# Linear attention and a gated MLP on one core: another order of norm multiplies, keys and gate differences in slabs 1 and 2, and of the Silu table load

## The chip, the cores and the metric

The kernel runs on one core of a Trainium2 chip. The metric is device time in microseconds (us), from the first to the last instruction of one launch, as the median of three runs. The profile is one execution of the same program; its span, 272.4 us, is a little shorter than the timed runs.

The engines that matter here are TensorE (PE, the matmuls, with PEld for its weight loads), VectorE (DVE), ScalarE (ACT, activations and copies), GpSimd (POOL) and SyncE (SP), whose queue issues most of the DMA transfers.

## The reference

Attention without a score matrix: the queries are normalized along the head dimension, the keys along the sequence, and keys times values is a 64x64 matrix for each head. A two-layer MLP with a gate `h * sigmoid(beta * h)` follows.

```python
def _attn_ref(q, k, v):                      # (8, 8, 576, 64) each
    q_s = np.exp(q - np.max(q, axis=-1, keepdims=True))
    q_s = q_s / (np.sum(q_s, axis=-1, keepdims=True) + 1e-09)
    k_s = np.exp(k - np.max(k, axis=2, keepdims=True))
    k_s = k_s / (np.sum(k_s, axis=2, keepdims=True) + 1e-09)
    kv = np.einsum('bhsd,bhse->bhde', k_s, v)
    return np.einsum('bhsd,bhde->bhse', q_s, kv)

def _moe_ref(x, w_in, w_out, beta):          # x (4608, 512), d_ff 2048
    h = x @ w_in
    g = h * (1.0 / (1.0 + np.exp(-beta * h)))
    return g @ w_out
```

(The listing writes exp and the subtraction of the maximum in one line; the inputs are 0.1 times normal values. The MLP's x is the attention output with the heads side by side.)

## The kernel before

The program is a list of operations, each given to an engine; `add` works out which earlier operations it must wait for, from the data that it reads (`r`), writes (`w`) and the PSUM banks that it touches. Operations of one engine run in the order in which they are listed. So the place of a call in the Python text is its place in the engine's queue.

The 4608 tokens are worked in nine slabs of 512: slab t for t = 0 to 7 is the first 512 tokens of batch t, and slab 8 the rest of all batches. In a slab, the first pass makes h from XT and WIN in 16 tiles of 128 features (64 matmuls); ScalarE applies Silu to each, and VectorE divides by beta (`scale_g`, line 767). The second pass multiplies by WOUT. It saves an eighth of the work with seven products in place of eight, for which it needs sums and differences of halves of the gates (`g_sum1`, `g_sum2`, `g_diff`).

Beside slab t's products, the attention of batch t + 1 is done. Here are its parts that matter: the norm of the queries (reduction, reciprocal, multiply), the DMA that transposes the result, the keys times values, and the product of both, `quad`.

```python
        def norm_main(b, hp0, n, eng=DVE, sums=True, mult=True):
            i = b % 2
            a = bass.AP(EQ[i], hp0 * 512, [[2048, 128], [64, 8 * n], [1, 64]])
            s_ = bass.AP(QS[i], hp0 * 8, [[32, 128], [1, 8 * n]])
            v_ = bass.AP(QI[i], hp0 * 8, [[32, 128], [1, 8 * n]])
            vb = bass.AP(QI[i], hp0 * 8, [[32, 128], [1, 8 * n], [0, 64]])
            ks = [("eq", i, hp) for hp in range(hp0, hp0 + n)]
            if sums:
                add(DVE, lambda e: e.tensor_reduce(s_, a, AX.X, ALU.add), r=ks,
                    w=[("qs", i, hp0)])
                add(DVE, lambda e: e.reciprocal(v_, s_), r=[("qs", i, hp0)], w=[("qi", i, hp0)])
            if mult:
                add(eng, lambda e: e.tensor_tensor(a, a, vb, ALU.mult), r=ks + [("qi", i, hp0)],
                    w=ks)
        # ... cut ...
        def kvd_t(b, c, n, bk):
            i = b % 2
            a = bass.AP(PS[bk], 0, [[512, 128], [256, n], [1, D]])
            rc = bass.AP(RC[i], c, [[NHP, 128], [1, n], [0, D]])
            add(DVE, lambda e: e.tensor_tensor(KVD[kd(b)][:, c:c + n, 0:D], a, rc, ALU.mult),
                r=[("ps", bk)] + [("rc", i, h2) for h2 in range(c, c + n)],
                w=[("kvd", kd(b), h2) for h2 in range(c, c + n)], bank=[bk])
        # ... cut: kv_steps(b, hps) issues PE's products of EK and VB, and then on VectorE:
                    c, k_ = hps[0], len(hps)
                    s_ = bass.AP(PS[bk], D, [[512, 128], [256, k_]])
                    add(DVE, lambda e: e.reciprocal(RC[i][:, c:c + k_], s_),
                        r=[("ps", bk)], w=[("rc", i, h2) for h2 in hps], bank=[bk])
                    if tiled(b):
                        kvd_t(b, c, k_, bk)
                        return
        # ... cut: quad(b, gs) makes XT for two (or four) of the four head pairs on PE (line 554) ...
            for x in sorted(b_x):
                eng, bk = (DVE, ACTE)[x % 2], b_x[x]
                add(eng, lambda e, eng=eng, x=x, bk=bk: (
                    e.copy if eng == ACTE else e.tensor_copy)(XT[i][:, x, :], PS[bk][:, :]),
                    r=[("ps", bk)], w=[("xt", i, x)], bank=[bk])
        # ... cut ...
        def turn(b, hp0, n):
            i = b % 2
            o = bass.AP(QT[i], hp0 * 512, [[2048, 128], [128, 4 * n], [1, 128]])
            a = bass.AP(EQ[i], hp0 * 512, [[2048, 128], [1, 512 * n]])
            add(SP, lambda e: e.dma_start_transpose(o, a),
                r=[("eq", i, hp) for hp in range(hp0, hp0 + n)],
                w=[("qt", i, hp) for hp in range(hp0, hp0 + n)], slot=f"tq{i}{hp0}")
        # ... cut ...
        def norm_turn(b, hp0):
            norm_main(b, hp0, 2, POOL)
            turn(b, hp0, 2)
        # ... cut ...
        def attn_late(b):
            if b < 4:
                return [(100 if b == 2 else 97, steps(kv_all, b)), (118, one(quad, b, (0,)))]
            return [(96, steps(kv_all, b)), (99, lambda: g_diff(1)), (112, one(quad, b))]
```

PE's matmuls for `quad` wait for KVD and for QT, so for the multiply as well, through the transpose. The gate differences are done in place on VectorE:

```python
        def g_diff(fh):
            f, th = NG * fh, 1 - fh
            add(DVE, lambda e: e.tensor_tensor(gv(f, th, NG), gv(f, th, NG), gv(f, 1 - th, NG),
                                               ALU.subtract),
                r=gk(f, 0, NG) + gk(f, 1, NG), w=gk(f, th, NG), war=True)
```

The second pass, with `at(n)` as the places at which a slab's hooks are called. `tick` counts PE's progress in the slab: 64 in the first pass, then 32/56 for each matmul of the second, so that product n (from 0) begins at 64 + 9.14 n. What `todo` holds is issued when its count is reached.

```python
            at(0)
        # ... cut ...
            prod_s(range(0, 6))
            prod(z5, *gs2(0), *wo(1, 1), True, False, range(0, 6))
            prod_s(range(6, NG))
            prod(z5, *gs2(0), *wo(1, 1), True, False, range(6, NG))
            add(DVE, lambda e: e.tensor_copy(TS[:, :], PS[s][:, :]), r=[("ps", s)], w=["ts"],
                bank=[s])
            at(1)
            add(DVE, lambda e: e.tensor_tensor(TS[:, :], TS[:, :], PS[z5][:, :], ALU.subtract),
                r=["ts", ("ps", z5)], w=["ts"], bank=[z5])
            at(2)
            prod(z2, *gs2(1), *wo(0, 0), True)
        # ... cut: VectorE subtracts z2 from TS (line 922) ...
            if t > 3:
                g_diff(0)
                g_diff(1)
            at(3)
            prod(z5, *gt(0, 0), *wo(0, 1), False)
            copy(z5, 0, 1, ACTE)
            at(4)
            prod(z2, *gt(NG, 1), *wo(1, 0), False)
            copy(z2, 1, 0, ACTE)
            at(5)
            prod(z5, *gt(0, 1), *wsum(1), False, True)
            last(z5, 1, 1)
            at(6)
            prod(z2, *gt(NG, 0), *wsum(2), False, True)
            last(z2, 0, 0)
            at(7)
```

`g_diff(0)` writes what the product after `at(5)` reads, `g_diff(1)` what the product after `at(6)` reads. z5 and z2 are two PSUM banks: a product can start in one of them when the copy before it has read it.

What a slab holds in `todo` (the second half of `quad` comes in the next slab, after its first product), and the hooks of slabs 1, 2 and 3 with `diffs_norm`:

```python
            elif t < 4:
                todo = attn_late(t + 1)
                if t > 1:
                    todo += [(1.5, one(quad, t, (1,)))]
        # ... cut ...
            def diffs_norm(b):
                norm_main(b, 2, 2, mult=False)
                g_diff(0)
                g_diff(1)
                norm_main(b, 2, 2, sums=False)
                turn(b, 2, 2)
        # ... cut ...
            if t == 1:
                on(0, exps, 2)
                on(0, casts, 2)
                on(2, norm_turn, 2, 0)
                on(3, diffs_norm, 2)
                on(3, load, 4)
            elif t == 2:
                on(0, exps, 3)
                on(2, norm_turn, 3, 0)
                on(3, diffs_norm, 3)
                on(3, load, 5)
                on(4, exp_q, 4)
                on(4, casts, 4)
                on(6, norm_turn, 4, 0)
            elif t == 3:
        # ... cut ...
                on(3, g_diff, 0)
                on(4, norm_turn, 5, 0)
                on(5, norm_turn, 5, 2)
```

ScalarE's Exp and Silu lie in different function tables. A load is put in ahead of the first activation that needs the other table; in slabs 1 and 2 the first Silu after the Exps is that of the next slab's first tile.

Of the kernel before, what the change touches and what calls it, by code (L numbers as in the profile page):

```python
# [7 lines left out]
ACT = mybir.ActivationFunctionType  # L8
# [21 lines left out]
PE, ACTE, DVE, POOL, SP = "tensor", "scalar", "vector", "gpsimd", "sync"  # L30
# [14 lines left out]
class Program:  # L45
# [12 lines left out]
    def add(self, eng, fn, r=(), w=(), bank=(), slot=None, after=(), war=False):  # L58
        op = Op(eng, fn, slot)
        op.pos = len(self.ops)  # L60
        deps = op.deps
        deps.extend(after)
        for k in r:
            deps.extend(self.writer.get(k, ()))
            self.readers.setdefault(k, []).append(op)
        for k in w:
            for d in self.readers.get(k, ()):
                if d is not op and (war or not self._same(d, op)):
                    deps.append(d)
            for d in self.writer.get(k, ()):  # L70
                if not self._same(d, op):
                    deps.append(d)
            self.readers[k] = []
            self.writer[k] = [op]
        for k in bank:
            t = self.touch.setdefault(k, {})
            for e, d in t.items():
                if e != eng:
                    deps.append(d)
            t[eng] = op  # L80
        if eng == POOL and slot is None:
            if self.pool is not None:
                deps.append(self.pool)
            self.pool = op
        self.ops.append(op)
        return op
# [72 lines left out]
def bass_efficient_attn_shen__then__act_swish_beta_kernel(  # L159
# [12 lines left out]
    with ExitStack() as es:  # L172
        def sb(name, shape, dt):
            return es.enter_context(nc.sbuf_tensor(name, shape, dt))
# [42 lines left out]
        WARM = sb("WARM", [128, 512], BF16)  # L217
        DUMMY = sb("DUMMY", [128, 8], F32)
# [7 lines left out]
        add = P.add  # L226
# [6 lines left out]
            r=["ts"], w=["idb"])  # L233
        add(POOL, lambda e: e.tensor_scalar(IDF[:, :], TS[0:NF, 0:NF], 0.0, None, ALU.is_equal),
            r=["ts"], w=["idf"])
        add(ACTE, lambda e: e.dma_start(BT[:, :], bass.AP(beta_h, 0, [[128, NF], [1, 128]])),
            w=["bt"], slot="bt")
        add(ACTE, lambda e: e.activation(DUMMY[:, 0:1], WARM[:, 0:1], ACT.Exp), r=["warm"],
            w=["dummy"])
# [109 lines left out]
# [14 lines that stand above are left out]
# [239 lines left out]
# [7 lines that stand above are left out]
# [14 lines left out]
        def one(fn, *a):  # L623
            return lambda: fn(*a)

        def steps(fn, *a):
            return lambda: go(fn(*a))
# [7 lines left out]

        def attn_late(b):
            if b < 4:
                return [(100 if b == 2 else 97, steps(kv_all, b)), (118, one(quad, b, (0,)))]
            return [(96, steps(kv_all, b)), (99, lambda: g_diff(1)), (112, one(quad, b))]

        def spread(steps, lo, hi):
# [9 lines left out]
        def go(steps):  # L651
            for s in steps:
                s()
# [18 lines left out]
        def load_wout(c):  # L672
# [11 lines left out]
            r=[("ps", bb)], w=["bc0"], bank=[bb])  # L684
        add(DVE, lambda e: e.scalar_tensor_tensor(BC[:, :], PS[bb][:, 0:NF], 1e-20, BC[:, :],
                                                  ALU.is_lt, ALU.mult),
            r=[("ps", bb), "bc0"], w=["bc"], bank=[bb])
        add(DVE, lambda e: e.scalar_tensor_tensor(BETA[:, :], BC[:, :], 4e-20, PS[bb][:, 0:NF],
                                                  ALU.mult, ALU.add),
            r=["bc", ("ps", bb)], w=["beta"], bank=[bb])  # L690
# [8 lines left out]
        for c in range(4):  # L699
# [33 lines left out]
            w=["dummy"])  # L733
# [57 lines left out]
        def gv(f, th, n):  # L791
            return GT[:, f:f + n, 256 * th:256 * th + 256]

        def gk(f, th, n):
            return [("gt", f + x, th) for x in range(n)]
# [12 lines left out]
# [5 lines that stand above are left out]
# [140 lines left out]
        for t in range(NSLAB):  # L953
            todo = []
            if t == 0:
                todo = [(x, steps(t_steps, 1, (hp,), NOW, ACTE))
                        for hp, x in enumerate((97, 106, 114, 119))]
                todo += [(107, one(exp_kr_s, 1))]
                todo += [(x, one(exp_k, 1, hp, 1)) for hp, x in enumerate((108, 115, 120, 125.5))]
                todo += [(x, one(cast_v, 1, hp, DVE))  # L960
                         for hp, x in ((1, 118.5), (2, 123), (3, 127))]
                todo += [(x, steps(kv_steps, 1, (hp,), NOW))
                         for hp, x in enumerate((118, 122, 126))]
                todo += [(x, steps(out_step, 1, hp, NOW, ACTE)) for hp, x in enumerate((122.5, 125))]
                todo += [(117, one(o2_evac, 0, 0, 3, ACTE))]
                todo += [(2, steps(out_step, 0, 3, HEAD, DVE))]
# [4 lines that stand above are left out]
                if t == 3:  # L971
                    todo += [(4, one(norm_turn, 4, 2))]
                if t == 1:
                    todo += [(1, steps(out_step, 1, 2, (3,), ACTE)),
                             (3, steps(kv_steps, 1, (3,), (7,))),
                             (6, steps(out_step, 1, 3, (7,), DVE)),
                             (6.1, one(w_sum, 2, 4, 4)), (6.2, one(w_diff, 0)),
                             (6.3, one(w_diff, 1))]
            elif t < 7:
                todo = attn(t + 1)  # L980
            elif t == 7:
                todo = spread(outr_steps(1), 32, 48)
# [31 lines left out]
            if t == 0:  # L1014
# [17 lines left out]
                while todo:  # L1032
# [4 lines left out]
                    r=["warm"], w=["dummy"])  # L1037
# [4 lines left out]
            def on(n, fn, *a):  # L1042
                hooks.setdefault(n, []).append(lambda: fn(*a))
# [4 lines left out]
                if b % 2 == 0:  # L1048
                    exp_kr(b)

            def diffs_norm(b):
                norm_main(b, 2, 2, mult=False)
                g_diff(0)
                g_diff(1)
                norm_main(b, 2, 2, sums=False)
                turn(b, 2, 2)

            def casts(b):
                g = P.writer[("gs2", NG - 1)]
# [5 lines left out]
            if t == 1:  # L1065
                on(0, exps, 2)
                on(0, casts, 2)
                on(2, norm_turn, 2, 0)
                on(3, diffs_norm, 2)
                on(3, load, 4)  # L1070
            elif t == 2:
                on(0, exps, 3)
                on(2, norm_turn, 3, 0)
                on(3, diffs_norm, 3)
                on(3, load, 5)
                on(4, exp_q, 4)
                on(4, casts, 4)
                on(6, norm_turn, 4, 0)
            elif t == 3:
                on(0, exp_k, 4)  # L1080
                on(0, exp_kr, 4)
                on(0, exp_q, 5)
# [3 lines that stand above are left out]
                on(4, exp_qr, 1)  # L1086
                on(5, exp_k, 5)
                on(5, norm_turn_rem)
                on(5, casts, 5)
                on(5, load, 6)  # L1090
                on(7, load_rem, "qrf", qt_h, QRF, 4)
            elif t + 2 < B:
                b = t + 2
                on(0, exps, b)
                on(0, casts, b)
                if t == 4:
                    on(0, load, 7)
                on(3, norm_turn, b, 0)
                on(4, norm_turn, b, 2)
# [40 lines left out]
```

## Time and profile before

| | |
|---|---|
| time, median of 3 | 274.03 us |
| lowest, highest | 273.77, 274.29 us |
| profile's span | 272.4 us |
| PE busy | 262.3 us (96%) |
| DVE busy | 193.9 us (71%) |
| ACT busy | 180.8 us (66%) |
| POOL busy | 58.8 us (22%) |
| granted PE clock | 1.000 |

The profile names an instruction by its line in the kernel and by what it writes and reads, with the numbers of buffers left out: `L361 POOL TENSOR_TENSOR EQ<-EQ,QI` is a norm multiply on GpSimd, `L361 DVE ...` one on VectorE, `L810 DVE ... GT<-GT` a gate difference, `L606 SPq DMA_TRANSPOSE QT<-EQ` the issue of a transpose. A group's idle time is the time in which its engine did nothing just before it, with the operation that ended it as the releaser. A busy time with xN is of N instructions taken together; neighbours on one engine overlap by up to 0.1 us. PE's records overlap more, since matmuls are pipelined.

Over the kernel's span ScalarE makes 16 table loads of 1283 ns each: six ahead of a Silu of line 744, six ahead of an Exp of line 319, and four single ones.

### The profile page before, as it was taken

Reading aid. Unit: us, or ns where it says so; the run is one execution under the profiler, and the core shown is the slowest. Engines: PE = TensorE matmul, PEld = TensorE weight load, DVE = VectorE, ACT = ScalarE, POOL = GpSimd, SP = SyncE. Lnnn points to the kernel's source line nnn. Section 1 sums busy time; section 2 is a strip of 40 time slices with the busy share of each in tenths; the row PEclk is TensorE's granted clock in tenths of the full one; section 3 lists DMA queues with packets and bytes.
Section 4 is the critical chain, followed back from the end, with each engine's and each line's share of the span. In section 5 each row is a group of like instructions: output and inputs, shape, how many; then the busy total and the mean of one; then the engine's idle time right before and its main releaser. Section 6 shows DMA issues by size and latency. Waiting matters only on the chain.

```text
span 272.4 us, 4985 instructions
## 1 busy us (share of the span) xinstructions
PE 262.3 (96%) x1974; PEld 163.5 (60%) x1993; DVE 193.9 (71%) x409; ACT 180.8 (66%) x287; POOL 58.8 (22%) x78
## 2 busy tenths in 40 slices
PE   8999999999899989999999999999999999999994
PEld 2444454448744864468645874587458745874683
DVE  4964586887958798868778885888488549625762
ACT  4898568789277955887778938893783387018610
POOL 2790010006130086100820651036000100000000
PEclk9999999999999999999999999999999999999999
DMA  7999999989799228960399899603600130012005
GB/s 219 318 201 207 227 326 350 288 236 370 157 328 285 82 42 231 293 211 2 63 261 298 252 359 162 193 1 79 213 2 0 22 154 0 2 58 99 0 2 155
DMA packets 59367, 45.95 MB, mean 169 GB/s; under 512 B 28608, under 2 KB 58320, under 8 KB 58320
## 3 DMA queue, kind: packets, MB, share of 16 engines
q1 hardware_dynamic: 54480, 40.90, 53.8%
q0 software_dynamic: 4240, 4.19, 9.3%
q10 hardware_dynamic: 624, 0.53, 0.6%
q8 instruction: 16, 0.26, 0.4%
q14 instruction: 7, 0.06, 0.1%
HBM read 36.71 MB, written 9.44 MB: 169 GB/s over the span
## 4 chain that ended last, share of the span: by engine, by line
PE 81%; DVE 12%; DMA 2%; SPq 2%; issue 1%; ACT 0%; DVEq 0%
PE PS L406 48%; PE PS L844 30%; DVE QS L357 3%; DMA VF<-in_v_dram 2%; DVE GT L810 2%; DVE EQ L361 2%; PE PS L554 1%; PE PS L482 1%; SPq L278 1%; SPq L290 1%; DVE QI L359 1%; DVE O2S L892 1%; DVE VB L377 1%; DVE TS L913 1%; DVE TS L916 1%
## 5 line engine op out<-in xcount | busy, mean ns | idle before, releaser
L406 PE MATMUL PS<-XT,WIN 128*128 128x512 bf16 x560 | 125.4, 379 | 1.5 <-issue 0.3
L744 ACT ACTIVATE GT<-PS,BETA 128x512 bf16<-128x512 f32 x144 | 95.0, 689 | 37.4 <-PE PS L406 37.2
L406 PEld LDWEIGHTS PS<-XT,WIN 128*128 128x128 bf16 x576 | 55.0, 98 | 65.2 <-DVE XT L596 1.1
L767 DVE TENSOR_SCALAR GT<-GT,RB 128x512 bf16<-128x512 bf16 x144 | 52.5, 386 | 38.4 <-ACT GT L744 37.7
L844 PE MATMUL PS<-WOUT,GS 128*128 128x256 bf16 x256 | 31.1, 273 | 0.0
L361 POOL TENSOR_TENSOR EQ<-EQ,QI 128x1024 bf16<-128x1024 bf16 (+1 forms) x11 | 20.0, 1822 | 50.5 <-DVE QI L359 50.2
L844 PE MATMUL PS<-WOUT,GT 128*128 128x256 bf16 x256 | 29.8, 273 | 0.0
L844 PE MATMUL PS<-WSUM,GT 128*128 128x256 bf16 x256 | 29.8, 273 | 0.0
L880 ACT COPY O2S<-PS 128x512 f32<-128x512 f32 (+1 forms) x17 | 9.4, 560 | 27.6 <-PE PS L844 27.6
L844 PEld LDWEIGHTS PS<-WSUM,GT 128*128 128x128 bf16 x256 | 24.8, 98 | 3.7 <-issue 0.9
L844 PEld LDWEIGHTS PS<-WOUT,GT 128*128 128x128 bf16 x256 | 24.8, 98 | 2.9
L844 PEld LDWEIGHTS PS<-WOUT,GS 128*128 128x128 bf16 x256 | 24.8, 98 | 3.0
L319 ACT ACTIVATE EQ<-QF 128x512 bf16<-128x512 f32 x32 | 17.9, 619 | 7.5 <-DMA QF<-in_q_dram 7.4
L803 DVE TENSOR_TENSOR GS<-GT 128x512 bf16<-128x512 bf16 (+2 forms) x32 | 21.9, 685 | 0.0
L377 POOL CAST VB<-VF 128x512 bf16<-128x512 f32 x24 | 16.4, 682 | 25.4 <-DVE GS L803 13.2
L810 DVE TENSOR_TENSOR GT<-GT 128x2048 bf16<-128x2048 bf16 x16 | 20.3, 1301 | 0.0
L357 DVE TENSOR_REDUCE QS<-EQ 128x16 f32<-128x1024 bf16 (+1 forms) x20 | 19.7, 985 | 0.7 <-ACT EQ L319 0.7
L319 ACT ACTIVATE EK<-KF 128x512 bf16<-128x512 f32 x32 | 18.1, 620 | 0.2 <-DMA KF<-in_k_dram 0.2
L892 DVE TENSOR_TENSOR O2S<-TS,PS 128x512 f32<-128x512 f32 (+1 forms) x17 | 10.7, 644 | 9.3 <-PE PS L844 9.3
L844 PE MATMUL PS<-WSUM,GS 128*128 128x256 bf16 x128 | 16.6, 273 | 0.0
L406 PE MATMUL PS<-WOUT,GT 128*128 128x512 bf16 x62 | 15.0, 379 | 0.1
L844 PEld LDWEIGHTS PS<-WSUM,GS 128*128 128x128 bf16 x128 | 12.5, 98 | 3.2
(88 smaller groups left out, 211.2 us busy)
## 6 DMA issues: line engine op xcount, KB each, us to landing
out_dram<-O2S SPq DMA_DIRECT2D x8, 1024.0 KB, 5.0
QF<-in_q_dram SPq DMA_DIRECT2D x6, 1024.0 KB, 6.7
KF<-in_k_dram SPq DMA_DIRECT2D x6, 1024.0 KB, 9.3
VF<-in_v_dram SPq DMA_DIRECT2D x6, 1024.0 KB, 12.5
KF<-in_k_dram SPq DMA_DIRECT2D x8, 256.0 KB, 5.5
VF<-in_v_dram SPq DMA_DIRECT2D x8, 256.0 KB, 5.5
WOUT<-in_moe_w_out_dram POOLq DMA_DIRECT2D x4, 512.0 KB, 16.4
WIN<-in_moe_w_in_dram POOLq DMA_DIRECT2D x3, 512.0 KB, 9.1
```

What stands on the lines that cost most here:

```text
L319: add(ACTE, lambda e, o=o, a=a: e.activation(o, a, ACT.Exp), r=[(name + "f", i, hp)], w=[("e" + name, i, hp)])
L357: add(DVE, lambda e: e.tensor_reduce(s_, a, AX.X, ALU.add), r=ks, w=[("qs", i, hp0)])
L361: add(eng, lambda e: e.tensor_tensor(a, a, vb, ALU.mult), r=ks + [("qi", i, hp0)], w=ks)
L377: add(eng, lambda e: (e.copy if eng == ACTE else e.tensor_copy)(o, a), r=[("vf", i, hp), ("vone", i)], w=[("vb", i, hp)], after=after)
L406: add(PE, lambda e: e.matmul(o, l, r_, start=start, stop=stop), r=r, w=w, bank=[bk])
L744: add(ACTE, lambda e: e.activation(GT[:, f, :], PS[bk][:, :], ACT.Silu, scale=BETA[:, f:f + 1]), r=[("ps", bk), "beta"], w=[("gt", f, 0), ...
L767: add(DVE, lambda e: e.tensor_scalar(GT[:, f, :], GT[:, f, :], RB[:, f:f + 1], None, ALU.mult), r=k + ["rb"], w=k)
L803: add(DVE, lambda e: e.tensor_tensor(GS2[:, i:i + n, :], GT[:, i:i + n, :], GT[:, i + NG:i + NG + n, :], ALU.add), r=[k_ for f in (i, i + ...
L810: add(DVE, lambda e: e.tensor_tensor(gv(f, th, NG), gv(f, th, NG), gv(f, 1 - th, NG), ALU.subtract), r=gk(f, 0, NG) + gk(f, 1, NG), w=gk(f ...
L844: add(PE, lambda e, l=l, r_=r_, st=st, u=u, i=i, b_=b_: e.matmul(PS[b_][:, 256 * u:256 * u + 256], l, r_, start=st, stop=end and i == NG - ...
L880: add(eng, lambda e, b_=b_, u0=u0, u1=u1: (e.copy if eng == ACTE else e.tensor_copy)(o[:, u0:u1, :], bank3(b_)[:, u0:u1, :]), r=[("ps", b_ ...
L892: add(DVE, lambda e, b_=b_, u0=u0, u1=u1: e.tensor_tensor(o[:, u0:u1, :], ts[:, u0:u1, :], bank3(b_)[:, u0:u1, :], ALU.add), r=["ts", ("ps ...
```

## The change

In slabs 1 and 2, VectorE now does the reductions and reciprocals of all four head pairs and the first gate difference, and no multiply; both multiplies of the norm go to GpSimd. The keys (`kv_all`: reciprocals and scaling into KVD) then come on VectorE ahead of the second gate difference, which moves into the list of `attn_late`, right after them. It is meant to bring KVD, and with it `quad`, earlier, by taking work out of VectorE's queue ahead of it.

A dummy activation with Silu is put in at `at(4)`, so that the table is loaded there, ahead of the output copy that follows, and not ahead of the next slab's first Silu. In slab 2 it comes after the four Exps of batch 4's queries. Slab 3 and all later ones have the same operations in the same order as before.

```diff
--- before.py
+++ after.py
@@ -635,7 +635,9 @@
 
         def attn_late(b):
             if b < 4:
-                return [(100 if b == 2 else 97, steps(kv_all, b)), (118, one(quad, b, (0,)))]
+                x = 100 if b == 2 else 97
+                return [(x, steps(kv_all, b)), (x + .1, lambda: g_diff(1)),
+                        (118, one(quad, b, (0,)))]
             return [(96, steps(kv_all, b)), (99, lambda: g_diff(1)), (112, one(quad, b))]
 
         def spread(steps, lo, hi):
@@ -1048,12 +1050,9 @@
                 if b % 2 == 0:
                     exp_kr(b)
 
-            def diffs_norm(b):
-                norm_main(b, 2, 2, mult=False)
-                g_diff(0)
-                g_diff(1)
-                norm_main(b, 2, 2, sums=False)
-                turn(b, 2, 2)
+            def silu_table():
+                add(ACTE, lambda e: e.activation(DUMMY[:, 2:3], WARM[:, 0:1], ACT.Silu),
+                    r=["warm"], w=["dummy"])
 
             def casts(b):
                 g = P.writer[("gs2", NG - 1)]
@@ -1066,14 +1065,18 @@
                 on(0, exps, 2)
                 on(0, casts, 2)
                 on(2, norm_turn, 2, 0)
-                on(3, diffs_norm, 2)
+                on(3, norm_turn, 2, 2)
+                on(3, g_diff, 0)
+                on(4, silu_table)
                 on(3, load, 4)
             elif t == 2:
                 on(0, exps, 3)
                 on(2, norm_turn, 3, 0)
-                on(3, diffs_norm, 3)
+                on(3, norm_turn, 3, 2)
+                on(3, g_diff, 0)
                 on(3, load, 5)
                 on(4, exp_q, 4)
+                on(4, silu_table)
                 on(4, casts, 4)
                 on(6, norm_turn, 4, 0)
             elif t == 3:
```

## The prediction

> **What bounds the kernel now.** I read the page first. In its busy times TensorE (PE) is busy for 262.3 us of 272.4, at a granted clock of 1.000, so all that a change of order can win back is the time in which PE stands still. Then I listed PE's waits over the whole span, and PE's timeline in the second passes of slabs 1 and 2 (60.9 to 75.3 us and 89.7 to 104.8 us). Columns: start, length, engine, line, what; the bracket is the idle time ahead of it and what ended it.
>
> ```profile
> 73.05 0.41 PE L554 MATMUL PS<-QT,KVD 64*64 64x512 bf16 x4 [0.97 <-DVE KVD L459]
> ...
> 102.47 0.41 PE L554 MATMUL PS<-QT,KVD 64*64 64x512 bf16 x4 [1.55 <-DVE RC L490]
> ...
> 106.82 3.41 PE L406 MATMUL PS<-XT,WIN 128*128 128x512 bf16 x15 [0.23 <-DVE XT L596]
> ```
>
> The three gaps, 0.97 + 1.55 + 0.23 = 2.75 us, are the whole prize. The first two stand before the first half of `quad` (L554), which needs both KVD (keys times values, scaled on VectorE) and QT (the transposed query factors, brought by DMA). The chain of waits through slab 2 shows why KVD is late: the two gate differences (L810) and the norm multiply (L361) stand ahead of it on VectorE (DVE).
>
> ```profile
> 97.65 2.72 DVE GT L810 x2
> 100.37 1.55 DVE EQ L361
> 101.92 0.09 DVE RC L490
> ...
> 102.04 0.29 DVE KVD L459
> 102.33 0.09 DVE RC L490
> ```
>
> Last I looked at the other input, QT, in the waits of two stretches, 72 to 74 us (first fence) and 101 to 103 us (second).
>
> ```profile
> PEld PS L554 <- DMA QT<-EQ: 1.2, 1, 1.2
> PE PS L554 <- DVE KVD L459: 1.0, 1, 1.0
> ```
>
> ```profile
> PEld PS L554 <- issue: 1.8, 1, 1.8
> PE PS L554 <- DVE RC L490: 1.5, 1, 1.5
> ```
>
> This is the reading that my number hangs on. In slab 1 the weight load of `quad` waited for the transposing DMA: it was issued at 68.92 and took 4.1 us to land, so at 73.02; KVD was done at 72.77 + 0.29 = 73.06. **Two inputs arrive within 0.05 us of each other**, and the change moves one of them. In slab 2 the transpose was issued at 97.77 and landed 3.1 us later, at 100.87, so there KVD alone holds PE.
>
> **What the skill says.** "SBUF — State Buffer", section "SBUF: two separate sides", says that VectorE and GpSimd share one port pair under an exclusive lock: a VectorE operation with two SBUF inputs, or in a 2-port mode, and a GpSimd operation shut each other out for a whole instruction. The trace agrees. POOL is GpSimd; the two lines are of POOL's and DVE's timelines:
>
> ```profile
> 108.32 1.90 POOL L361 TENSOR_TENSOR EQ<-EQ,QI 128x1024 bf16<-128x1024 bf16 x1 [0.65 <-DVE QI L359]
> ```
>
> ```profile
> 108.61 1.75 DVE L767 TENSOR_SCALAR GT<-GT,RB 128x512 bf16<-128x512 bf16 x1 [0.44 <-ACT GT L744]
> ```
>
> The scaling that takes 386 ns on average took 1.75 us, and ended as the GpSimd multiply did. "ScalarE: Activation LUTs", section "What ACT_TABLE_LOAD costs", puts a switch at 2.66 us with its drain; here the load is 1.28 us and the next activation follows at once (120.25 to the first Exp at 121.55: 1.30), so I use 1.30. Its section "Table sets: the hidden batching unit" says that cheap functions such as copy are in every set; the trace agrees: the copies of L880 run after Exp and those of L771 between Silus with no load of their own.
>
> **The change part by part.**
>
> *1. The multiply leaves DVE.* In each of slabs 1 and 2 one multiply of 128x1024 goes: 1.14 us of the chain in slab 1 (1.21 with overlap), 1.55 in slab 2 (there it waited behind a GpSimd cast). On GpSimd the same shape takes 1.90 us (four of them, 67.0 to 108.3).
>
> *2. The second difference goes behind the keys.* That takes another 1.15 us from ahead of KVD. The tail of reciprocals and scalings is unchanged: 72.25 to 73.06 in slab 1, so 0.81 us, once started.
>
> *3. New order in slab 1.* Up to 68.80 (end of the second reciprocal L359) nothing differs. GpSimd's first multiply ends at 68.90, as before. The first difference starts at 68.72, ahead of the second multiply, which can start some 0.1 us after the first; so I take it that DVE gets the port first, and ends at 69.98 as before. Keys: from 69.9 plus 0.9 to 70.8. The second multiply held the port from 69.9 for 1.85 us to 71.75; the second difference then runs until about 72.85. KVD is thus 2.2 us earlier, **but QT still lands at 73.02**, since the first multiply and the first transpose haven't moved. `quad` starts at 73.05 as before. The second difference at 72.85 is in time for the last product, which started at about 73.5. **Gain of slab 1: 0.** (The second transpose is issued at about 71.8 in place of 72.28; nobody waits for that.)
>
> *4. New order in slab 2.* The reciprocal ends at 97.65. First difference, with the port, to 98.82 (as now). Keys to 99.65. The second multiply blocked until 98.75, then to 100.6. The second difference from 100.6 to 101.7. GpSimd's casts, now behind the multiply, run from 100.7 on and end at about 105.6 in place of 104.4, ahead of the next multiply; that one is not urgent. `quad` needs KVD (99.65), QT (100.87) and PE's own fifteen products before it (from 99.13, 1.80 long: 100.93). So it starts at about 101.0 in place of 102.47: 1.45 us earlier.
>
> *5. What then holds the last product.* After `quad` (0.35) and one product of the sixth group PE would reach the last group at about 101.45. It needs the second difference (101.7) and its PSUM bank, which is free when ScalarE's second output copy has read it. Here is ScalarE (ACT) in slab 2 before:
>
> ```profile
> 98.29 2.19 ACT L319 ACTIVATE EQ<-QF 128x512 bf16<-128x512 f32 x4
> 100.38 0.57 ACT L880 COPY O2S<-PS 128x512 f32<-128x512 f32 x1
> ...
> 106.35 1.28 ACT L744 ACT_TABLE_LOAD   x1
> 107.89 0.69 ACT L744 ACTIVATE GT<-PS,BETA 128x512 bf16<-128x512 f32 x1 [0.26 <-PE PS L406]
> ```
>
> The table load now stands between these four Exps and the copy. Exps end at 100.48, load to 101.78, the dummy of 0.20 to 101.98; the copy of 0.57, overlapping it by 0.1, from 101.9 to 102.47. So the last group starts at about 102.5, in place of 102.93 (102.82 and one product of 0.11). **Gain 0.43 us, not 1.45**: one wait takes the place of the other, for 1.0 us.
>
> *6. The start of slab 3.* With the last group 0.43 us earlier, PE reaches the second half of `quad` at about 104.8. Ahead of its cast on DVE stand the first cast (101.7 to 102.4), an addition (to 103.0), a reduction and its reciprocal (to 104.4) and an addition (to 105.1); the cast then ends at 105.8, when PE has four products of slab 3 behind it (105.15 + 0.86 = 106.0). The gap of 0.23 goes. **Gain 0.23.**
>
> *7. The table load itself.* In slab 2's start the first Silu came right behind the load (76.93 + 1.28 = 78.21, Silu at 78.22), so Silus begin perhaps 0.2 us earlier; but PE runs without a gap from 76.13 to 89.70, so that is worth 0. At slab 3's start the Silu waited for PE anyway (idle 0.26 after the load). In slab 1 the moved load lies in ScalarE's idle stretch between its two copies, 68.46 to 70.48 (2.02 us idle; 1.5 needed). **Gain 0.** The number of loads stays the same.
>
> Sum: 0 + 0.43 + 0.23 + 0 = 0.66 us. From 107 us on, PE is the chain almost without a break (only 0.05 and 0.16 at a time is lost), so nothing later should swallow it: 274.03 - 0.66 = **273.4 us**.
>
> **The rivals.** *A: the whole prize.* If PE is released by KVD in both slabs and the copy isn't late, 2.75 us go, to 271.3 us. For it: both gaps bear a DVE name. Against: the landing at 73.02 and the copy behind the load. A half version, in which the copy doesn't hold the bank as I work out but the difference does (101.75), gives slab 2 about 1.2 + 0.2 = 1.4: 272.6 us. *B: the port turns against it.* If GpSimd's second multiply gets the lock first, the first difference ends near 72.0 in slab 1, KVD at 72.9, the second difference only at 74.0: the last group waits 0.5 us there, and in slab 2 the second difference ends at about 102.8 in place of 101.7. Slab 1 then loses 0.5 and slab 2 gains 0.2 at most: 274.3 us. Against: the difference starts some 0.2 us before the multiply can. *C: nothing.* The gaps stay filled by other waits, or the casts displaced on GpSimd delay the next slab's multiplies and through the port the scalings behind them (the 1.75 above): 274.0 us. Against: that multiply at 108.32 would still end earlier, since its companion starts at 105.7.
>
> **Range and chances.** My sum is 273.4; B and C lie at 274.3 and 274.0, the half of A at 272.6, and three runs of the kernel before lie between 273.77 and 274.29, so 0.3 to either side is measurement. I take 272.6 to 274.2. Two per cent are 5.5 us, twice the whole prize; none of the rivals reaches it either way, so 0.98 for within 2%, and 0.01 for each side.
>
> **What would show it.** Right: in slab 1 `quad` still at 73.05, its idle time now ended by the DMA of QT; in slab 2 `quad` at about 101.0, then a new idle time of PE of about 1 us before the last WSUM<-GT group, ended by ScalarE's copy L880; the second multiply of GpSimd 2.7 us long, with the wait for the port in it; no 0.23 at the start of slab 3; first Silus with no load ahead of them. Wrong: `quad` of slab 1 before 72.8; no wait for the copy; or a first difference (L810) of 2 us or more.

## The result and the profile after

The changed kernel takes 272.82 us (median of six; 272.47 to 273.43), the kernel before 274.23 us beside it (273.77 to 274.57). The ratio is **0.9953, 95% interval 0.9937 to 0.9968**: 1.4 us faster. In a second comparison it was 272.84 us at 0.9958 (0.9938 to 0.9978). The profile's span went from 272.4 to 271.1 us.

The three places at which PE stood still, in PE's timeline of the changed kernel (columns as above; all its line numbers past 640 are two higher than in the kernel before):

```profile
70.28 1.80 PE L846 MATMUL PS<-WSUM,GT 128*128 128x256 bf16 x15
72.11 0.41 PE L554 MATMUL PS<-QT,KVD 64*64 64x512 bf16 x4
...
72.96 1.91 PE L846 MATMUL PS<-WSUM,GT 128*128 128x256 bf16 x16 [0.23 <-DVE GT L812]
...
98.57 1.80 PE L846 MATMUL PS<-WSUM,GT 128*128 128x256 bf16 x15
100.35 0.41 PE L554 MATMUL PS<-QT,KVD 64*64 64x512 bf16 x4
...
101.97 1.92 PE L846 MATMUL PS<-WSUM,GT 128*128 128x256 bf16 x16 [0.99 <-ACT O2S L882]
...
104.59 7.74 PE L406 MATMUL PS<-XT,WIN 128*128 128x512 bf16 x35
```

Neither `quad` has idle time ahead of it any more. Two waits have moved behind it, ahead of the last product group: 0.23 us for the second difference in slab 1, 0.99 us for ScalarE's output copy in slab 2. The 0.23 at the start of slab 3 is gone: a run without a break from 104.59.

The chain of waits through slab 2 now runs through ScalarE and no more through VectorE:

```profile
97.25 0.59 ACT O2S L882
97.83 2.09 ACT EQ L319 x4
99.92 0.02 issue
99.94 1.28 ACT L1054
101.22 0.01 issue
101.23 0.20 ACT DUMMY L1054
101.44 0.48 ACT O2S L882
101.92 0.05 issue
101.97 1.92 PE PS L846 x16
```

L1054 is the Silu table load at its new place. The copy behind it could have run at 99.9. On VectorE (first fence) and GpSimd (second) the sequence in slab 1 reads:

```profile
68.71 1.26 DVE L812 TENSOR_TENSOR GT<-GT 128x2048 bf16<-128x2048 bf16 x1
...
70.09 0.29 DVE L459 TENSOR_TENSOR KVD<-PS,RC 128x128 bf16<-128x128 f32 x1
...
70.70 2.12 DVE L812 TENSOR_TENSOR GT<-GT 128x2048 bf16<-128x2048 bf16 x1
```

```profile
66.99 4.74 POOL L361 TENSOR_TENSOR EQ<-EQ,QI 128x1024 bf16<-128x1024 bf16 x2
```

The two multiplies take 4.74 us in place of 2 x 1.90, and the second difference 2.12 in place of 1.2: each waited some 0.9 us for the other's turn, but the keys in between waited for nobody.

**One table for all runs.** Absolute times shift by up to 0.4 us between executions, since the head of the kernel does. So I count from the start of the fifteen WSUM<-GT products ahead of `quad` in the same slab: to `quad`, and to the first product of the last group (where a record runs on as x17, the first of it still belongs to the group before, and the last group starts 0.11 later). The fifth column is the first break in slab 3's first matmuls after `quad`, between two starts, less their usual 0.22.

| profile | slab 1: to `quad` | slab 1: to last group | slab 2: to last group | break in slab 3 | time, us |
|---|---|---|---|---|---|
| before (of the prediction) | 2.77 | 3.23 | 3.80 | 0.39 | 274.23 |
| before, second profile | 2.52 | 2.97 | 3.79 | 0.39 | 274.58 |
| before, third profile | 2.51 | 2.97 | 3.80 | 0.39 | 274.31 |
| changed | 1.83 | 2.68 | 3.40 | 0 | 272.82 |
| changed, second profile | 1.83 | 2.69 | 3.39 | 0 | 272.84 |
| no table loads moved | 1.84 | 2.68 | 2.68 | 0.18 | 272.72 |
| slab 2's load behind the copy | 2.45 | 2.90 | 2.68 | 0.18 | 272.36 |
| table loads alone | 2.52 | 2.97 | 3.80 | 0.39 | 273.83 |
| multiplies to GpSimd alone | 3.09 | 3.55 | 3.54 | 0.39 | 274.64 |
| keys between alone | 2.14 | 2.92 | 3.68 | 0.18 | 274.02 |

Against the second and third profiles of before, the change is worth 0.29 in slab 1, 0.40 in slab 2 and 0.39 at the start of slab 3: 1.08 us of the 1.4 that the clock shows.

**Where the rest lies.** Each timed execution also has its span, and so a time outside the span. The next table has the two distances to the last groups and the break added up, less before; the median span; and the median of time less span.

| kernel | three added, less before | span, us | time less span, us |
|---|---|---|---|
| before (19 executions; 11 others) | 0 | 272.1; 272.2 | 2.16; 2.15 |
| changed (two comparisons) | -1.08; -1.08 | 271.0; 271.0 | 1.81; 1.81 |
| no table loads moved | -1.62 | 270.6 | 2.15 |
| slab 2's load behind the copy | -1.40 | 270.6 | 1.77 |
| table loads alone | 0 | 272.0 | 1.83 |
| multiplies to GpSimd alone | +0.32 | 272.5 | 2.16 |
| keys between alone | -0.38 | 271.8 | 2.17 |

The spans follow the distances to within 0.2 us. Time less span falls into two groups: 1.76 to 1.92 us in the three kernels with the moved table loads (29 of 30 executions; one has 2.57), 2.09 to 2.42 in every execution of the others. So some 0.35 us of the change's gain come with the two moved loads and lie outside the span; with the 1.08 they make the 1.4. What happens there no run shows.

### The profile page after: what moved, and what is told of

It is laid out like the page before. It is cut to its first block, busy times and chain, and to the rows that moved or that the text cites. A ratio compares the mean times of both kernels' runs of the same rounds, so it can differ in the third digit from the quotient of the medians.

```text
span 271.1 us, 4991 instructions
## 1 busy us (share of the span) xinstructions
PE 262.9 (97%) x1974; PEld 163.7 (60%) x1993; DVE 192.1 (71%) x407; ACT 181.5 (67%) x289; POOL 64.0 (24%) x80
## 4 chain that ended last, share of the span: by engine, by line
PE 85%; DVE 7%; DMA 2%; ACT 2%; SPq 2%; issue 1%; DVEq 0%
PE PS L406 49%; PE PS L846 33%; DMA VF<-in_v_dram 2%; DVE QS L357 2%; PE PS L482 1%; PE PS L554 1%; DVE GT L812 1%; SPq L278 1%; SPq L290 1%; ACT EQ L319 1%; DVE EQ L361 1%; DVE VB L377 1%; DVE QI L359 0%; ACT L1054 0%; ACT O2S L882 0%
## 5 line engine op out<-in xcount | busy, mean ns | idle before, releaser
L361 POOL TENSOR_TENSOR EQ<-EQ,QI 128x1024 bf16<-128x1024 bf16 (+1 forms) x13 | 25.6, 1968 | 47.2 <-DVE QI L359 46.5
L812 DVE TENSOR_TENSOR GT<-GT 128x2048 bf16<-128x2048 bf16 x16 | 21.4, 1362 | 0.0
```

## The experiments

**1. The kernel before, profiled again.** No edit.

> The kernel before, unchanged, for a second profile. The first transpose of slab 1 (issued at 68.92 us) landed after 4.1 us in the profile of before and after 3.1 us in that of the changed kernel, with the same instructions ahead of it. Theory A (one DMA engine was late in that one execution, nothing to do with the change): the landing varies, 3.1 to 4.1 us, while quad of slab 1 stays at 73.05 since KVD is done at 73.06. Theory B (the changed order makes the landing earlier): 4.1 us again. Time 274.2 under both.

274.58 us (one run). The transpose, now issued at 69.20, landed after 3.1 us, at 72.3 (first fence: its landing time); `quad` started at 73.08, 0.15 us after the *first* of the two scalings into KVD (second fence: VectorE's timeline), while the second one was still to come. PE's line is the third.

```profile
DMA to landing us min/median/max: 3.1/3.1/3.1
```

```profile
72.64 0.29 DVE L459 TENSOR_TENSOR KVD<-PS,RC 128x128 bf16<-128x128 f32 x1
72.84 0.16 DVE L490 RECIPROCAL RC<-PS 128x2 f32<-128x2 f32 x1
73.04 0.29 DVE L459 TENSOR_TENSOR KVD<-PS,RC 128x128 bf16<-128x128 f32 x1
```

```profile
73.08 0.41 PE L554 MATMUL PS<-QT,KVD 64*64 64x512 bf16 x4 [0.71 <-DVE RC L490]
```

Theory A holds for the landing, and B falls: over the ten profiles of this study it takes 3.1 to 4.1 us, whichever order follows. But A's second half is wrong in its reason: `quad` stood at nearly the same clock time by chance, for here PE's own work was 0.28 us later (the fifteen products started at 70.56, not 70.28) and the idle time fell from 0.97 to 0.71. The first half of `quad` reads head pairs 0 and 1 only, which the first scaling makes.

**2. The changed kernel without the two moved loads.**

```diff
-                on(4, silu_table)
```

(in slab 1 and in slab 2)

> The changed kernel without its two Silu table loads. Theory A (in slab 2 the moved load delays the second output copy, and that holds the last product group): the group starts 0.14 us after the second difference, at about 101.25 in place of 101.97, PE's idle time there falls from 0.99 to about 0.3; slab 1 unchanged; first Silus come no more than 0.2 us later and PE doesn't wait for them. Time 272.1, 0.7 below the changed kernel. Rival B (the early table load is what gains): slower than the changed kernel, 273.5 to 274.

272.72 us, ratio to before 0.9951 (0.9931 to 0.9970). The last group of slab 2 starts 0.72 us earlier (2.68 in place of 3.40), and what it waits for is now the second difference:

```profile
101.15 1.91 PE L846 MATMUL PS<-WSUM,GT 128*128 128x256 bf16 x16 [0.28 <-DVE GT L812]
```

Theory A's mechanism holds, and rival B falls: without the loads the kernel isn't slower. But the time went down by 0.1 us and not by the 0.7 expected: of the 0.72, 0.18 is lost again at slab 3's start (PE gets there sooner than XT), and the 0.35 us outside the span are gone with the loads. The six times spread from 272.16 to 274.22, so that by times alone this kernel and the changed one aren't told apart.

**3. Slab 2's load behind the second copy.**

```diff
                 on(4, exp_q, 4)
-                on(4, silu_table)
+                on(5, silu_table)
```

> The changed kernel, with slab 2's table load behind the second output copy in place of ahead of it (slab 1's stays). Theory A: as without the loads, last group of slab 2 at about 101.25, time 272.1. Theory B (what holds the last group is the second difference or PE's own order, and the copy only ends at the same time): same as the changed kernel, 272.8.

**272.36 us, ratio 0.9930 (0.9917 to 0.9943): the fastest of all.** ScalarE now has the copy first, and the load right behind it:

```profile
99.90 0.57 ACT L882 COPY O2S<-PS 128x512 f32<-128x512 f32 x1
100.49 1.28 ACT L1054 ACT_TABLE_LOAD   x1
```

The last group starts after 2.68, as without the loads. So the 0.7 us that slab 2 loses in the changed kernel is this one load's place. By its span (270.6 us, as in experiment 2) it is no better than experiment 2; the 0.36 us between their times lie outside the span, and the intervals overlap. This profile also caught a late transpose, 3.8 us to landing, and so shows what slab 1 does then:

```profile
72.57 0.41 PE L554 MATMUL PS<-QT,KVD 64*64 64x512 bf16 x4 [0.65 <-DMA QT<-EQ]
```

That is the wait that the prediction expected in slab 1. It comes and goes with the execution.

**4. The table loads alone.** The kernel before, with `silu_table` and its two hooks, in the places of the change; `diffs_norm` as before.

```diff
                 on(3, diffs_norm, 2)
+                on(4, silu_table)
 ...
                 on(4, exp_q, 4)
+                on(4, silu_table)
```

> The kernel before with the two Silu table loads alone, at the places that the change gives them; multiplies, keys and differences as before. Theory A: in slab 2 the second copy ends at about 102.5, still ahead of the last group at 102.93, and PE never waited for the first Silus; 274.2, no change. Rival B (the load at the slab's start cost something): 0.5 to 1 us faster, 273.5.

273.83 us, ratio 0.9984 (0.9971 to 0.9998). In the profile not one of the four distances differs from before, as theory A has it; from the first product of slab 1's second pass to the end the span is 211.38 us, and 211.48 and 211.43 in the second and third profiles of before. The times are 0.45 us lower, which A doesn't give and which is just short of what rival B asks. About 0.1 of it is in the span (272.0 against 272.1), the rest outside (1.83 against 2.16). So it is not a wait of the first Silus that went, as B supposed; whether the place of the loads or the two added activations do it stays open.

**5. The multiplies alone.** Both on GpSimd, both differences still ahead of the keys, no moved loads. The edit is against the changed kernel; the lines of slab 1 are shown, those of slab 2 are alike.

```diff
-                return [(x, steps(kv_all, b)), (x + .1, lambda: g_diff(1)),
-                        (118, one(quad, b, (0,)))]
+                return [(x, steps(kv_all, b)), (118, one(quad, b, (0,)))]
 ...
                 on(3, g_diff, 0)
+                on(3, g_diff, 1)
-                on(4, silu_table)
```

> Both multiplies on GpSimd, but both gate differences still ahead of the keys, and no moved table load. Theory A (a multiply on GpSimd and a difference on VectorE shut each other out, so taking the multiply off VectorE frees nothing while a difference behind it waits for it): the second difference takes 2.0 us or more, quad of slab 1 starts 0.5 us later than before relative to PE's work, quad of slab 2 0.2 us earlier; 274.5, no gain. Rival B (the multiply was simply removed from VectorE's queue): differences of 1.2 us each, quad about 1 us earlier in both slabs; 272.8 to 273.2.

274.64 us, ratio 1.0011 (0.9999 to 1.0024): **no gain at all.** The profile's distances make it 0.32 us slower. VectorE (L811 is the difference here) and GpSimd in slab 1:

```profile
68.70 4.10 DVE L811 TENSOR_TENSOR GT<-GT 128x2048 bf16<-128x2048 bf16 x2
72.72 0.16 DVE L490 RECIPROCAL RC<-PS 128x2 f32<-128x2 f32 x1
```

```profile
66.98 4.74 POOL L361 TENSOR_TENSOR EQ<-EQ,QI 128x1024 bf16<-128x1024 bf16 x2
```

Two differences take 4.10 us, 2.39 in the kernel before: the second waits until the multiply on GpSimd is through (71.72). The 1.2 us that left VectorE's queue come back as 1.7 us of waiting. `quad` of slab 1 comes 0.57 us later, that of slab 2 0.25 us earlier (3.09 in place of 3.34). Rival B falls.

**6. The keys alone.** The keys between the differences; the second multiply on VectorE ahead of them; no moved loads. The edit is against the changed kernel.

```diff
+            def diffs_norm(b):
+                norm_main(b, 2, 2, mult=False)
+                g_diff(0)
+                norm_main(b, 2, 2, sums=False)
+                turn(b, 2, 2)
 ...
-                on(3, norm_turn, 2, 2)
-                on(3, g_diff, 0)
-                on(4, silu_table)
+                on(3, diffs_norm, 2)
```

(and the same for slab 2)

> The keys between the two gate differences, the second multiply left on VectorE ahead of the keys, and no moved table load. Theory A: slab 1's quad is freed (about 1 us earlier) but the second difference ends later than in the changed kernel, at about 73.1 and 102.6, so the last groups start near where they did before; 273.8, a gain of about 0.4. Rival B (the order of the keys alone gives the gain): 272.7, as the changed kernel without the loads.

274.02 us, ratio 0.9986 (0.9973 to 0.9999): a fifth of the change's gain by the median, and at the edge of what the times can tell; the profile's distances give 0.38 us. KVD holds neither `quad` any more (slab 1's waits 0.34 us for QT, which landed after 3.5 us in this execution), but the second difference is now the last thing on VectorE, and PE waits for it in slab 2. Slab 1's `quad` and slab 2's last group:

```profile
72.53 0.41 PE L554 MATMUL PS<-QT,KVD 64*64 64x512 bf16 x4 [0.34 <-DMA QT<-EQ]
...
102.60 1.91 PE L846 MATMUL PS<-WSUM,GT 128*128 128x256 bf16 x16 [1.26 <-DVE GT L812]
```

Rival B falls, by more than 1 us. The parts don't add up: +0.3 and -0.3 us alone, -1.6 us together (experiment 2). Moved to GpSimd, the multiply runs its 1.9 us beside the keys, which don't need what it holds (their scalings take 0.29 us there as before), and only the second difference waits for its end; alone, either part leaves the differences and the multiply in one row ahead of the last group.

**7. The kernel before against itself.** No edit.

> The kernel before against itself, for what the measurement alone makes of two equal programs: ratio 1.000 within 0.002; if it comes out at 0.998, the 0.45 us of the two table loads alone are no finding.

Ratio 1.0000 (0.9988 to 1.0013). Differences of 0.5 us and more are the kernels'. The 0.45 of experiment 4 is at the edge of what the times tell, but its time less span (1.83 us) stands clear of both sides here (2.15).

**8. The changed kernel again.** No edit.

> The changed kernel, timed beside these: 272.8. In its profile, quad of slab 1 waits for the transposing DMA if that lands after 3.8 us or more, and doesn't if it lands after 3.1 us; the last group of slab 2 waits 1.0 us for the second output copy in either case.

272.84 us, ratio 0.9958 (0.9938 to 0.9978). The transpose landed after 3.1 us, `quad` of slab 1 had no idle time, and the last group of slab 2 waited again:

```profile
102.05 1.92 PE L846 MATMUL PS<-WSUM,GT 128*128 128x256 bf16 x16 [0.97 <-ACT O2S L882]
```

## Where the prediction was right and where it was wrong

The time lies in the range, near its lower end, and the direction is right; the gain was put at half its size (0.66 us against 1.4). The misses have one sign: 0.29 us in slab 1, 0.16 at the start of slab 3 and 0.35 outside the span. That the range still holds the time is in part luck: its lower end, 272.6, came from a rival whose reason fell.

- **Steps 1 and 2** (what leaves VectorE) hold, and so does the exclusive lock on the shared port that the Trainium skill states ("SBUF — State Buffer", section "SBUF: two separate sides"): in experiment 5 a difference waited 1.7 us for a multiply.
- **Step 3, "Gain of slab 1: 0", failed.** It was 0.29 us (0.55 against the prediction's own profile, with its late transpose). The text named its own test, "`quad` of slab 1 before 72.8", and `quad` started at 72.11. Two things were wrong in "two inputs arrive within 0.05 us of each other". The prediction took the landing of 4.1 us from a single execution for a property of the kernel; in six of the ten profiles it is 3.1 to 3.3, in the others 3.5 to 4.1. And it took the second scaling (73.06) for the one that `quad` waits for; it is the first (72.36 + 0.29 = 72.65). So KVD held `quad` in the two later profiles of before and in experiment 4, while in the first profile QT, at about 73.02, came some 0.37 us behind it. That half of rival A's argument was right. The rest of step 3 holds to 0.05 us: keys done at 70.8 (70.78), second multiply through at 71.75 (71.73), second difference at 72.85 (72.82). That difference is what keeps slab 1 from gaining more.
- **Step 4** holds: `quad` of slab 2 without a wait. At the prediction's clock, 0.56 us later than the profile's after slab 1, it stands at 100.91, against "about 101.0".
- **Step 5** holds, and it is the part of the prediction that could most easily have been missed: gain 0.40 against 0.43, the wait 0.99 against "about 1 us", with the copy named. Experiments 2 and 3 show it by taking it away.
- **Step 6** had the mechanism right and the size too small: 0.39 in place of 0.23. The idle time of PE counts from the modelled end of a matmul. A matmul of 512 columns is recorded as 0.38 us long, but in an unbroken run they start every 0.22 us; so a break with 0.23 us of idle time costs 0.23 + 0.38 - 0.22 = 0.39. The prize of 2.75 us was too small by the same 0.16; the two gaps ahead of `quad` were read nearly right (2.77 and 3.34 us from the start of the fifteen products, against 1.78 where nothing held it: 0.99 and 1.56).
- **Step 7, "Gain 0", holds** inside the span and not for the time: first Silus waited for PE (idle 1.17 us ahead of slab 2's, no load), and PE gained nothing by it, but the time fell by some 0.35 us outside the span (experiment 4). Why is open.

Of the rivals, A's half version (272.6) gave the better number, with the wrong reason: the copy does hold the bank. B didn't occur: the first difference got the port in both slabs and took 1.26 us. Nor did C, no gain: the interval ends at 0.9968.

The late QT of the first profile of before cost 0.25 us there (2.77 against 2.52), in that execution only.

## What to carry to other kernels

Moving work to an engine that shares a resource with the old one paid here only where what then stood next in the old queue didn't need that resource: the multiply paid when the keys, and not a gate difference, came to lie beside it. When a table load is moved into "idle" time, look at what stands behind it in the same queue: the idle stretch must be ahead of the next instruction that someone waits for. And where two inputs of a wait come within half a microsecond of each other in a profile, and one is a transfer, take a second profile before building on which is last. Last, compare times and spans separately: a gain that no profile shows may lie outside the span.

## What the runs showed of the hardware

The transpose of 128x1024 bf16 within SBUF took 3.1 to 4.1 us to land in ten executions with the same instructions ahead of it. A gate difference and a GpSimd multiply that meet take turns whole: 2.12 us in place of 1.2 for the one, 4.74 in place of 3.80 for two of the other; the scalings into KVD, which read PSUM, took 0.29 us beside a multiply as they did without one. And a wait on VectorE is to be read with the operand, not with the line: of two scalings of one line, the first was the one that counted.
